# Attention over two caches: one branch's scores turned to keys-by-queries, its row sums taken from a ones column that GpSimd puts beside V

## The chip, the cores and the metric

The kernel runs on one core of one Trainium2 chip. The metric is device time in microseconds, lower is better; the time before is 957.26 us, the median of three runs (957.25 to 958.89).

## What is computed

Two attention blocks, A and B, read their own activations, caches and weights, and their outputs stand side by side. A has 32 query heads on 4 cached heads (8 query heads share one K and V), B has 32 on 32.

```python
def _A_ref(x, k_cache, v_cache, wq, wo):          # B=16, Sq=32, D=1024, Sk=1024, Dh=128
    q = (x @ wq).reshape(B, Sq, Hq, Dh).transpose(0, 2, 1, 3)
    k = jnp.repeat(k_cache, rep, axis=1)          # A: 4 heads, rep = 8;  B: 32 heads, no repeat
    v = jnp.repeat(v_cache, rep, axis=1)
    scores = jnp.einsum("bhqd,bhkd->bhqk", q, k) * (Dh ** -0.5)
    p = _softmax(scores, axis=-1)
    o = jnp.einsum("bhqk,bhkd->bhqd", p, v)
    return o.transpose(0, 2, 1, 3).reshape(B, Sq, Hq * Dh) @ wo
...
return jnp.concatenate([a, b], axis=-1)
```

All tensors are bfloat16. B's K and V are 268 MB together, A's 34 MB, the four weight matrices 34 MB.

## The kernel before

Work is cut into steps, 128 for A and 128 for B. One step of B takes two batches and two heads: 128 rows of queries (2 x 2 x 32) against 1024 keys, with 1 MB of K (`KB_sb`, two buffers) and 1 MB of V (`VB_sb`, three buffers, two loads each). One step of A takes one batch and four of the eight query heads that share a cached head: again 128 rows of queries, on partitions, against 1024 keys. Two steps of A (`half` 0 and 1) use one K and one V of 256 KB (`KA_sb`, `VA_sb`, two buffers each).

A step of A runs so (function `quadA_all`):

1. K is transposed on TensorE through `ps_kt` and copied to `KTA_sb` (`st_ktrA`, L837), once for two steps, for the batch after.
2. `st_scores` (L860): Q is the stationary operand, K-transposed streams by: two matmuls of 512 columns give scores as queries by keys in `ps_s` (two buffers, shared with B).
3. `st_exp` (L899): ScalarE writes exp of the scores to `P_sb` and adds up the rows in `stat` on the way.
4. `st_ptr` (L913): four float32 transposes (two bfloat16 columns taken as one) turn P to keys by queries in `ps_pt`; `st_pev` copies that to `PT_sb` on ScalarE (L588, the helper `evac`).
5. `st_pv` (L931): eight matmuls, one per chunk of 128 keys, add up the output in `ps_o`.
6. `st_recip` (DVE, L950) and `st_norm` (ScalarE, L956) divide by the row sum, giving `O_sb`; `st_otr` transposes it in `ps_o` (L967), and DVE copies it to `OTA_sb` (L590).

B's steps do the same, with K transposed by DVE (`st_ktrB`, L846), scores in small tiles of 32x32 (L882), PV in tiles of 32 columns (L941), the division on DVE (L960) and the last copy on ScalarE. Projections of Q (L657, L674) and of the output (L735) run through the bank `ps_pj`, spread over the steps; sums over blocks of heads are kept in `acc` (L746, L748, L751).

PSUM has eight banks: four for `ps_s`, one each for `ps_kt`, `ps_pt`, `ps_o` and `ps_pj`. Before the change A and B share `ps_pt` and `ps_o`.

The order of instructions is not the order in which the code adds them. Each operation is recorded with what it reads and writes; `list_schedule` then replays all of them with a table of durations (`DUR`) and one figure for the transfer rate (`DMA_BW`), and sorts them by the start that this gives. On the chip each engine works through its own list in that fixed order, with semaphore waits where a buffer demands one. All loads are issued by SyncE (SP), also in a fixed order; a load that waits holds up those behind it. `A_STEPS_FRAC` places A's 128 steps in the first 92% of B's.

The program also holds a second, general version of the computation, which runs only if a check of the row sums fails (`emit_programs`).

Of the kernel before, what the change touches and what calls it, by code (L numbers as in the profile page):

```python
# [7 lines left out]
ALU = alu_op_type.AluOpType  # L8
# [10 lines left out]
A_O_IN_KT = False  # L19
# [16 lines left out]
    "KBt_tr": 1.15, "max": 1.17, "recip": 0.07, "norm@dve": 0.30, "PT_ev@dve": 0.62, "OT_ev@dve": 0.16, "KTA_ev@dve": 0.62,  # L36
# [449 lines left out]
def build(nc, pa, pb, out):  # L486
    P = 128
# [34 lines left out]
    with contextlib.ExitStack() as stack:  # L522
# [10 lines left out]
        stat = sb("stat", [P, 2, 4], F32)  # L533
# [34 lines left out]
        if A_O_IN_KT:  # L568
            OREG = [(ps_kt, BK_KT), (ps_o, BK_O)]
        else:  # L570
            OREG = [(ps_o, BK_O), (ps_o, BK_O)]
# [7 lines left out]
               reads=["z32"], writes=["id32"], name="c1")  # L579

# [141 lines left out]
        def oproj(pi, blk, G):  # L722
# [7 lines left out]
            for oh in range(NOH):  # L730
# [11 lines left out]
                o_ap = ost[:, pi, oh * OUTW:(oh + 1) * OUTW]  # L742
                if nblk == 1:
                    evac(o_ap, ps_pj[:, 0:OUTW], reads=[BK_PJ], writes=[BK_PJ, ("ost", pi)], name="o_fin")
# [15 lines left out]
        def mk_quadA(t):  # L760
# [15 lines left out]
            q.rinv = rinv_all[:, t:t + 1]  # L776
# [38 lines left out]
        def st_dmaV(q):  # L815
            if q.pi == 0:
# [3 lines left out]
                pr.add("sp", lambda e: e.dma_start(VA_sb[:, sl, :, :], pa["v"][q.b, q.s].rearrange("(p c) d -> p c d", c=NCH)),  # L820
# [70 lines left out]
        def st_exp(q):  # L891
# [4 lines left out]
            else:  # L896
# [287 lines left out]
```

## Time and profile before

| | before |
|---|---|
| median of 3 runs | 957.26 us |
| profiled execution | 959.08 us |
| its span | 957.3 us |
| granted TensorE clock, mean | 0.979 |
| busy: DVE / ACT / POOL | 503.5 / 576.0 / 1.3 us |
| DMA packets, share of 16 engines | 94.9% |
| HBM read / written | 337.64 / 2.10 MB |

PE stands for TensorE, PEld for its weight loads, DVE for VectorE, ACT for ScalarE, POOL for GpSimd, SP for SyncE. A row of a group reads: line, engine, operation, what is written and what is read, shape, count, then busy time in us and mean duration in ns, then the engine's idle time ahead of it and what ended most of that. The chain of waits is followed back from the last instruction to whatever released it. A row of waits reads: who waited, for what, us in total, times, the longest. The profile's span is the time from the first to the last instruction on the core.

### The profile page before, as it was taken

To read this page: it belongs to the slowest core of one execution; us is meant where nothing else is said; L and a number is where in the kernel's file an instruction comes from. 1 tells how busy PE (TensorE), PEld (TensorE's weight loads), DVE (VectorE), ACT (ScalarE), POOL (GpSimd) and SP (SyncE) were. 2 spreads that over 40 slices of the span, in tenths; PEclk is the share of its full clock that TensorE was granted. 3 is DMA by queue.
4 is the path that set the end of the run, shared out by engine and by line. 5 is a ranking of instruction groups with operands and counts; after the bars stand their busy time and mean duration, and the time that the engine had idled before them with its cause. 6 is when DMAs were issued, how large, how long until landed. Compare 5 with 4: busy or idle time off the path is not lost.

```text
span 957.3 us, 29084 instructions
## 1 busy us (share of the span) xinstructions
PE 850.0 (89%) x12866; PEld 473.5 (49%) x12866; DVE 503.5 (53%) x955; ACT 576.0 (60%) x1237; POOL 1.3 (0%) x10
## 2 busy tenths in 40 slices
PE   5889999999999899999999899999999988898775
PEld 3345555555555455555555455555555545454332
DVE  1434454545545565555554555654556555556643
ACT  2246676766666666757666666656677656666432
POOL 0000000000000000000000000000000000000000
PEclk7989999999999999999999999999999999999987
DMA  8889999999999999998999999999899999989995
GB/s 318 300 307 369 364 343 367 404 357 360 341 382 388 367 352 352 399 361 318 361 363 408 390 334 370 349 366 389 328 362 378 407 377 358 357 298 363 380 411 179
DMA packets 151938, 341.68 MB, mean 357 GB/s; under 512 B 10496, under 2 KB 26880, under 8 KB 151808
## 3 DMA queue, kind: packets, MB, share of 16 engines
q1 hardware_dynamic: 151808, 339.78, 94.9%
q8 instruction: 102, 1.67, 0.6%
q14 instruction: 28, 0.23, 0.1%
HBM read 337.64 MB, written 2.10 MB: 355 GB/s over the span
## 4 chain that ended last, share of the span: by engine, by line
PE 65%; ACT 24%; DVE 6%; issue 2%; DMA 2%; SPq 0%; POOLq 0%; DVEq 0%
PE ps_pt L913 14%; ACT P_sb L899 13%; PE ps_s L882 12%; PE ps_pj L735 9%; PE ps_o L941 7%; PE ps_pj L657 6%; ACT PT_sb L588 5%; PE ps_pj L674 5%; PE ps_o L931 5%; PE ps_s L860 3%; DVE KBt_sb L846 3%; PE ps_kt L837 2%; ACT QR L588 2%; ACT KTA_sb L588 1%; PE ps_o L967 1%
## 5 line engine op out<-in xcount | busy, mean ns | idle before, releaser
L846 DVE STREAM_TRANSPOSE KBt_sb<-KB_sb 128x1024 f32<-128x1024 f32 x256 | 308.3, 1225 | 38.3 <-PE ps_s L882 27.2
L899 ACT ACTIVATE P_sb<-ps_s 128x1024 bf16<-128x1024 f32 x256 | 263.8, 1030 | 83.3 <-PE ps_s L882 53.7
L588 ACT COPY PT_sb<-ps_pt 128x512 f32<-128x512 f32 x256 | 150.3, 587 | 190.3 <-PE ps_pt L913 169.9
L913 PE MATMUL ps_pt<-id,P_sb 128*128 128x128 f32 x1024 | 184.3, 303 | 24.1 <-ACT P_sb L899 19.5
L913 PEld LDWEIGHTS ps_pt<-id,P_sb 128*128 128x128 f32 x1024 | 147.4, 208 | 76.6 <-ACT P_sb L899 48.4
L882 PE MATMUL ps_s<-KBt_sb,QR 32*32 32x512 bf16 x4096 | 171.0, 400 | 10.5 <-ACT QR L588 8.5
L931 PE MATMUL ps_o<-VA_sb,PT_sb 128*128 128x128 bf16 x1024 | 80.2, 222 | 16.7 <-ACT OTB_sb L588 15.0
L960 DVE TENSOR_SCALAR O_sb<-ps_o,rinv_all 128x128 bf16<-128x128 f32 x128 | 44.1, 345 | 90.4 <-PE ps_o L941 89.7
L941 PEld LDWEIGHTS ps_o<-VB_sb,PT_sb 128*32 128x32 bf16 x4096 | 59.8, 97 | 60.9 <-issue 44.9
L941 PE MATMUL ps_o<-VB_sb,PT_sb 128*32 128x128 bf16 x4096 | 83.9, 222 | 4.9 <-DVE OTA_sb L590 1.8
L950 DVE RECIPROCAL rinv_all<-stat 128x1 f32<-128x1 f32 x256 | 37.9, 150 | 95.8 <-ACT P_sb L899 87.5
L860 PE MATMUL ps_s<-KTA_sb,QT_sb 128*128 128x512 bf16 x256 | 84.9, 384 | 3.6 <-ACT KTA_sb L588 2.0
L931 PEld LDWEIGHTS ps_o<-VA_sb,PT_sb 128*128 128x128 bf16 x1024 | 61.9, 99 | 49.2 <-ACT OTB_sb L588 33.6
L882 PEld LDWEIGHTS ps_s<-KBt_sb,QR 32*32 32x32 bf16 x4096 | 47.4, 89 | 76.9 <-issue 41.1
L735 PE MATMUL ps_pj<-woB_sb,OTB_sb 128*128 128x512 bf16 x256 | 73.1, 386 | 5.4 <-DVE ost L751 2.6
L590 DVE COPY OTA_sb<-ps_o 128x128 bf16<-128x128 bf16 x128 | 27.9, 218 | 93.4 <-PE ps_o L967 92.9
L674 PE MATMUL ps_pj<-wq_sb,xT_sb 128*128 128x512 bf16 x256 | 70.0, 387 | 3.9 <-DMA wq_sb<-in_B_wq_dram 1.7
L735 PE MATMUL ps_pj<-woA_sb,OTA_sb 128*128 128x512 bf16 x256 | 69.7, 380 | 3.4 <-DVE ost L751 1.3
L657 PE MATMUL ps_pj<-xT_sb,wq_sb 128*128 128x512 bf16 x256 | 67.9, 383 | 4.1 <-ACT QR L588 1.3
L748 DVE TENSOR_TENSOR acc<-acc,ps_pj 128x512 f32<-128x512 f32 x64 | 43.8, 684 | 48.9 <-PE ps_pj L735 48.8
L588 ACT CAST QR<-ps_pj 128x256 bf16<-128x256 f32 x128 | 48.5, 379 | 24.0 <-PE ps_pj L694 23.3
L967 PE MATMUL ps_o<-ident,O_sb 128*128 128x128 bf16 x256 | 56.9, 222 | 5.3 <-DVE O_sb L960 2.7
(46 smaller groups left out, 552.2 us busy)
## 6 DMA issues: line engine op xcount, KB each, us to landing
KB_sb<-in_B_k_cache_dram SPq DMA_DIRECT2D x128, 1024.0 KB, 6.9
VB_sb<-in_B_v_cache_dram SPq DMA_DIRECT2D x256, 512.0 KB, 8.0
KA_sb<-in_A_k_cache_dram SPq DMA_DIRECT2D x64, 256.0 KB, 7.2
VA_sb<-in_A_v_cache_dram SPq DMA_DIRECT2D x64, 256.0 KB, 6.5
wq_sb<-in_B_wq_dram SPq DMA_DIRECT2D x32, 256.0 KB, 7.3
wq_sb<-in_A_wq_dram SPq DMA_DIRECT2D x32, 256.0 KB, 7.5
woB_sb<-in_B_wo_dram SPq DMA_DIRECT2D x32, 256.0 KB, 7.7
woA_sb<-in_A_wo_dram SPq DMA_DIRECT2D x32, 256.0 KB, 8.1
```

Of the source, the lines that this page charges most:

```text
L588: pr.add("act", lambda e: e.copy(dst_ap, src_ap), reads=reads, writes=writes, name=name + "@act", wtag=wtag, rtag=rtag)
L657: last = e.matmul(ps_pj[:, 0:tn], wq_sb[:, 0, j, hc * Dh:(hc + 1) * Dh], xT_sb[:, 0, j, t0:t0 + tn], start=(j == 0), stop=(j == DJ - 1))
L674: last = e.matmul(ps_pj[:, 0:CW], xT_sb[:, 1, j, G * P:(G + 1) * P], wq_sb[:, 1, j, :], start=(j == 0), stop=(j == DJ - 1))
L735: last = e.matmul(ps_pj[:, 0:OUTW], OT[:, gp, hh, :], wo_[:, hh, oh * OUTW:(oh + 1) * OUTW], start=(hh == 0), stop=(hh == nh - 1))
L846: pr.add("dve", lambda e: e.transpose(KBt_sb[:, sl, t_, :].bitcast(F32), KB_sb[:, rs, t_, :].bitcast(F32)), reads=[("KB", rs)], writes=[(" ...
L860: pr.add("pe", lambda e, u=u: e.matmul(ps_s[:, sbf, u, :], qt[:, q.b, q.hh0:q.hh0 + 4, :].rearrange("p a q -> p (a q)"), KTA_sb[:, sl, u * ...
L882: last = e.matmul(ps_s[32 * cg:32 * cg + 32, sbf, g2, :].rearrange("p (s j) -> p s j", s=16), lhsT, rhs, start=(fp == 0), stop=(fp == 3), ...
L899: pr.add("act", lambda e: e.activation(dst, src, ACTF.Exp, scale=scale, accum_out=stat[:, sl, 1:2]), writes=BK_S[sbf] + [("P", sl), ("rows ...
L913: last = e.transpose(ps_pt32[:, m * P:(m + 1) * P], p32[:, m:Sk // 2:NPK], id32[:])
L931: last = e.matmul(OREG[0][0][:, 0:Dh], ptc, VA_sb[:, kvs, c, :], start=(c == 0), stop=(c == NCH - 1))
L941: last = e.matmul(ps_o[32 * a:32 * a + 32, 0:Dh], ptc, VB_sb[:, kvs, a // 2, a % 2, c, :], start=(c == 0), stop=(c == NCH - 1), tile_posit ...
L967: pr.add("pe", lambda e: e.transpose(ot_ps, O_sb[:, sl, :], ident[:]), reads=[("O", sl), "ident"], writes=[OREG[q.pi][1]], name="OT_tr", r ...
```

## The change

A's step is cut another way. A step is now one batch, all eight query heads (256 rows of queries) and half of the keys (`half` selects 512 of 1024). K-transposed is the stationary operand and Q streams by, so that scores arrive as keys by queries; exp writes them straight to `PTA_sb` in bfloat16, in the form that PV reads. The transposes `PT_trA`, the copy `PT_ev` and the accumulator of exp are gone for A. V of A is loaded to one buffer `VA_sb`; GpSimd copies it to `VAp_sb` (two buffers), whose rows have 128 columns of V and a column of ones that is set once. PV has 129 columns; the last one is the row sum. Both steps of a batch add up in `ps_kt`; after the second one `st_finA` divides on DVE (reciprocal and product), transposes twice on TensorE and copies once on DVE to `OTA_sb`. A no longer uses `ps_pt` and `ps_o`. B keeps its steps; its `P_sb`, `PT_sb`, `stat` and O lose the index that told A and B apart, as does `ost`, which both now share. Four heads of A's first Q projection (`pro_heads`) come one step of A earlier. The table `DUR` is altered with it.

```diff
 DUR = {
-    "scoresB": 1.1, "scoresA": 0.45, "PT_trA": 0.50, "PT_trB": 0.50, "PVA": 0.48, "PVB": 0.8, "OT_tr": 0.10, "KTA_tr": 0.50,
+    "scoresB": 1.1, "scoresA": 0.45, "PT_trB": 0.50, "PVB": 0.8, "OT_tr": 0.10, "KTA_tr": 0.50,
...
-    "exp": 1.12, "PT_ev@act": 0.52, "norm@act": 0.46, "OT_ev@act": 0.24, "KTA_ev@act": 0.93, "qA_ev@act": 0.52, "qB_ev@act": 0.52,
+    "exp": 1.25, "expA": 1.05, "VAp_cp": 1.2, "normA@dve": 0.42, "OT_trA": 0.2, "OT_evA@dve": 0.35, "PT_ev@act": 0.52, "norm@act": 0.46, "OT_ev@act": 0.24, "KTA_ev@act": 0.93, "qA_ev@act": 0.52, "qB_ev@act": 0.52,
...
-        VA_sb = sb("VA_sb", [P, 2, NCH, Dh], BF)
+        VA_sb = sb("VA_sb", [P, NCH, Dh], BF)
...
+        PTA_sb = sb("PTA_sb", [P, 2, NCH // 2, 2 * P], BF)
+        VAp_sb = sb("VAp_sb", [P, 2, NCH, Dh + 2], BF)
...
+        for i in range(2):
+            pr.add("pool", lambda g, i=i: g.memset(VAp_sb[:, i, :, Dh:Dh + 1], 1.0), writes=[("VAp", i)], name="c0")
...
-                pr.add("sp", lambda e: e.dma_start(VA_sb[:, sl, :, :], pa["v"][q.b, q.s].rearrange("(p c) d -> p c d", c=NCH)),
-                       writes=[("VA", sl)], dma_key=f"va{sl}", name="va_dma", dur=Sk * Dh * 2, wtag={("VA", sl): q.kid})
+                pr.add("sp", lambda e: e.dma_start(VA_sb[:, :, :], pa["v"][q.b, q.s].rearrange("(p c) d -> p c d", c=NCH)),
+                       writes=["VA"], dma_key="va", name="va_dma", dur=Sk * Dh * 2, wtag={"VA": q.kid})
+                pr.add("pool", lambda g: g.tensor_copy(VAp_sb[:, sl, :, 0:Dh], VA_sb[:, :, :]), reads=["VA"], writes=[("VAp", sl)], name="VAp_cp",
+                       rtag={"VA": q.kid}, wtag={("VAp", sl): q.kid})
...
+                qt = QT_sb[:, q.s % 2, q.b, :, :].rearrange("p a q -> p (a q)")
+
+                for c2 in range(2):
+                    def e_st(e, c2=c2):
+                        for i in range(2):
+                            c = 4 * q.half + 2 * c2 + i
+                            last = e.matmul(ps_s[:, sbf, c2, i * 2 * P:(i + 1) * 2 * P], KTA_sb[:, sl, c * P:(c + 1) * P], qt, start=True, stop=True)
+                        return last
...
+                dst = PTA_sb[:, q.half, :, :].rearrange("p c n -> p (c n)")
+                pr.add("act", lambda e: e.activation(dst, src, ACTF.Exp, scale=scale),
+                       writes=BK_S[sbf] + [("PTA", q.half)], name="expA",
...
+        def st_pvA(q):
+            sl, h = q.kvslot, q.half
+
+            def e_pv(e, c0):
+                for c in range(c0, c0 + 2):
+                    for qh in range(2):
+                        last = e.matmul(ps_kt[:, qh * OA0:qh * OA0 + Dh + 1], PTA_sb[:, h, c, qh * P:(qh + 1) * P], VAp_sb[:, sl, 4 * h + c, 0:Dh + 1],
+                                        start=(h == 0 and c == 0 and qh == 0), stop=(h == 1 and c == 3), skip_group_check=True)
+                return last
...
+        def st_finA(q):
+            o2 = ps_kt[:, 0:2 * OA0].rearrange("p (h n) -> p h n", h=2)
+            rinv = rinv_all[:, 2 * q.u:2 * q.u + 2]
+            pr.add("dve", lambda e: e.reciprocal(rinv.rearrange("p (h n) -> p h n", n=1), o2[:, :, Dh:Dh + 1]), reads=[], writes=[BK_KT, "rinvA", ("rinv_all", 0)],
+                   name="recip", rtag={"OpsA": q.kid}, wtag={"rinvA": q.kid})
+            pr.add("dve", lambda e: e.tensor_tensor(OA_sb[:, :, :], o2[:, :, 0:Dh], rinv.rearrange("p (h n) -> p h n", n=1).broadcast_to([P, 2, Dh]), ALU.mult),
+                   reads=["rinvA"], writes=[BK_KT, "OA"], name="normA@dve", rtag={"rinvA": q.kid, "OpsA": q.kid}, wtag={"OA": q.kid})
...
             st_scores(q)
             st_exp(q)
-            st_ptr(q)
-            st_pev(q, "act")
-            st_pv(q)
-            st_recip(q)
-            st_norm(q, "act")
-            st_otr(q, "dve")
+            st_pvA(q)
+            if q.half == 1:
+                st_finA(q)
```

What stands in the engines' lists is set by the replay, so here are rows of those lists: line, operation, what is written and read, shape, and how many of the kind follow each other. First PE before, somewhat before the middle of the program: L882 are B's scores, L941 B's PV, L860 A's scores, L931 A's PV, L913 the transposes of P for A or B, L967 those of O, L657 and L674 Q projections.

```order
L882 MATMUL ps_s<-KBt_sb,QR 32x512 x8
L931 MATMUL ps_o<-VA_sb,PT_sb 128x128 x8
L657 MATMUL ps_pj<-xT_sb,wq_sb 128x512 x2
L913 MATMUL ps_pt<-id,P_sb 128x128 x4
L860 MATMUL ps_s<-KTA_sb,QT_sb 128x512 x2
L967 MATMUL ps_o<-ident,O_sb 128x128
L657 MATMUL ps_pj<-xT_sb,wq_sb 128x512 x6
L882 MATMUL ps_s<-KBt_sb,QR 32x512 x24
L941 MATMUL ps_o<-VB_sb,PT_sb 32x128 x32
L913 MATMUL ps_pt<-id,P_sb 128x128 x4
```

One step of A stands between B's scores. In the changed kernel, at a like place, A's scores are L865, its PV L937, its output transposes L955, K's transposes L839; B's are L887, L971, L992 and L921.

```order
L839 MATMUL ps_kt<-ident,KA_sb 128x128 x8
L674 MATMUL ps_pj<-wq_sb,xT_sb 128x512 x2
L865 MATMUL ps_s<-QT_sb,KTA_sb 128x256 x4
L674 MATMUL ps_pj<-wq_sb,xT_sb 128x512 x2
L971 MATMUL ps_o<-VB_sb,PT_sb 32x128 x32
L937 MATMUL ps_kt<-VAp_sb,PTA_sb 128x129 x8
L992 MATMUL ps_o<-ident,OB_sb 128x128
L937 MATMUL ps_kt<-VAp_sb,PTA_sb 128x129 x8
L865 MATMUL ps_s<-QT_sb,KTA_sb 128x256 x4
L735 MATMUL ps_pj<-woB_sb,OTB_sb 128x512 x2
L955 MATMUL ps_kt<-ident,OA_sb 128x128 x2
L865 MATMUL ps_s<-QT_sb,KTA_sb 128x256 x4
```

No transposes of P are left for A, and three steps of A's scores stand here with no scores of B between them. A dozen rows further on, still on PE of the changed kernel:

```order
L887 MATMUL ps_s<-KBt_sb,QR 32x512 x32
L735 MATMUL ps_pj<-woA_sb,OTA_sb 128x512 x8
L971 MATMUL ps_o<-VB_sb,PT_sb 32x128 x32
L887 MATMUL ps_s<-KBt_sb,QR 32x512 x32
L735 MATMUL ps_pj<-woA_sb,OTA_sb 128x512 x2
L921 MATMUL ps_pt<-id,P_sb 128x128 x4
```

Here two steps of B follow each other with none of A. Last, SP's list, before, with the semaphores that a load waits for in brackets:

```order
L813 DMA KB_sb<-in_B_k_cache_dram 128x2x2048 [waits s_dve]
L808 DMA KA_sb<-in_A_k_cache_dram 128x1024
L826 DMA VB_sb<-in_B_v_cache_dram 128x2x1024 x2
L813 DMA KB_sb<-in_B_k_cache_dram 128x2x2048 [waits s_dve]
L820 DMA VA_sb<-in_A_v_cache_dram 128x1024
L826 DMA VB_sb<-in_B_v_cache_dram 128x2x1024 x2
```

And SP's list of the changed kernel:

```order
L808 DMA KA_sb<-in_A_k_cache_dram 128x1024 [waits s_pe]
L813 DMA KB_sb<-in_B_k_cache_dram 128x2x2048
L820 DMA VA_sb<-in_A_v_cache_dram 128x1024 [waits s_pool]
L813 DMA KB_sb<-in_B_k_cache_dram 128x2x2048 [waits s_dve]
L828 DMA VB_sb<-in_B_v_cache_dram 128x2x1024 [waits s_pe]
L828 DMA VB_sb<-in_B_v_cache_dram 128x2x1024
L808 DMA KA_sb<-in_A_k_cache_dram 128x1024 [waits s_pe]
L820 DMA VA_sb<-in_A_v_cache_dram 128x1024 [waits s_pool]
```

Loads of VA_sb now wait for GpSimd (`s_pool`), and between the two of them stand one load of KB_sb, two of VB_sb and one of KA_sb.

More of the change, by code (lines that the diff above doesn't have):

```diff
@@ L775, in mk_quadA @@
             q.qid = ("A", t)
-            q.rinv = rinv_all[:, t:t + 1]
+            q.u = t // 2
             q.kid = ("A", q.s, q.b)
@@ new lines, in st_pv, with e_pv @@
+        def st_pv(q):
+            kvs = q.vslot
+            def e_pv(e, c0):
+                last = None
+                for c in range(c0, c0 + 2):
+                    for a in range(4):
+                        last = e.matmul(ps_o[32 * a:32 * a + 32, 0:Dh], PT_pairs[:, c // 2, 32 * a:32 * a + 32, c % 2], VB_sb[:, kvs, a // 2, a % 2, c, :],
+                                        start=(c == 0), stop=(c == NCH - 1), tile_position=(0, 32 * a))
+                return last
+            for c0 in range(0, NCH, 2):
+                pr.add("pe", lambda e, c0=c0: e_pv(e, c0), reads=["PT", ("VB", kvs, 0), ("VB", kvs, 1)], writes=[BK_O], name="PVB",
+                       dur=0.2, tag="B%d" % q.t, rtag={"PT": q.qid, ("VB", kvs, 0): q.kid, ("VB", kvs, 1): q.kid}, wtag={"Ops": q.qid})
```

153 lines of the change are left out of this document (59 added, 94 removed).

## The prediction

> **What bounds the kernel now.** I read the busy shares first, then the chain that ended last, then the DMA figures, then all of it by stage.
>
> ```profile
> PE 850.0 (89%) x12866; PEld 473.5 (49%) x12866; DVE 503.5 (53%) x955; ACT 576.0 (60%) x1237; POOL 1.3 (0%) x10
> PE 65%; ACT 24%; DVE 6%; issue 2%; DMA 2%; SPq 0%; POOLq 0%; DVEq 0%
> DMA packets 151938, 341.68 MB, mean 357 GB/s; under 512 B 10496, under 2 KB 26880, under 8 KB 151808
> ```
>
> The first line says that TensorE is busy for 89% of the span and no other compute engine for more than 60%. The second, the chain, runs over PE, ACT and DVE for 95% of the time; transfers end a wait in only 2% of it. So today compute sets the pace. The third line is the warning: 341.68 MB move at 357 GB/s on average, so the queue has not much room either. Three stages and three selected stretches show how much (columns: window, its length, busy us of PE, PEld, DVE, ACT and POOL, then granted clock, DMA share, GB/s):
>
> ```profile
> 0.00:100.00 100.00, 78.42 (x868) 41.05 (x869) 36.46 (x63) 41.95 (x84) 1.18 (x9) 0.90 0.90 327
> 100.00:900.00 800.00, 734.77 (x11288) 414.88 (x11286) 440.99 (x845) 513.92 (x1106) 0.00 (x0) 1.00 0.97 364
> 900.00:957.30 57.30, 36.76 (x713) 17.59 (x713) 26.07 (x49) 20.14 (x47) 0.10 (x1) 0.86 0.82 313
> ...
> 290.00:330.00 40.00, 37.10 (x569) 20.29 (x568) 20.51 (x42) 23.39 (x51) 0.00 (x0) 1.00 1.04 406
> 490.00:530.00 40.00, 36.88 (x544) 21.23 (x544) 21.04 (x42) 25.61 (x58) 0.00 (x0) 1.00 1.05 406
> 735.00:765.00 30.00, 27.51 (x412) 15.12 (x411) 16.98 (x34) 19.63 (x45) 0.00 (x0) 1.00 1.05 407
> ```
>
> The steady stage is 100 to 900. There PE is busy 734.77 of 800 us and idle 65.2, and the queue moves 364 GB/s x 800 us = 291 MB. In three stretches of 30 to 40 us it holds 406 to 407 GB/s, so 406 is a rate that these transfers can sustain. At 406 the steady stage's bytes take 800 x 364 / 406 = **717 us**. Two resources thus stand close together: PE at 735, DMA at 717, and the stage takes 800 because neither is always fed. Start (x and the first weights) and end (B alone, A's steps being over) are stages of their own, and A's attention hardly touches them.
>
> **The change, part by part.** First what leaves PE, ACT and DVE.
>
> ```profile
> L913 PE MATMUL ps_pt<-id,P_sb 128*128 128x128 f32 x1024 | 184.3, 303 | 24.1 <-ACT P_sb L899 19.5 <-ACT PT_sb L588 2.1
> 100.00:900.00 800.00, 166.39 (x932) 133.46 (x930) 1.00 0.97 364
> ...
> L931 PE MATMUL ps_o<-VA_sb,PT_sb 128*128 128x128 bf16 x1024 | 80.2, 222 | 16.7 <-ACT OTB_sb L588 15.0 <-DVE rinv_all L950 1.0 <-DVE OTA_sb L590 0.2
> L860 PE MATMUL ps_s<-KTA_sb,QT_sb 128*128 128x512 bf16 x256 | 84.9, 384 | 3.6 <-ACT KTA_sb L588 2.0 <-DVE QT_sb L590 0.8 <-ACT QT_sb L588 0.7
> 100.00:900.00 800.00, 79.05 (x240) 20.84 (x240) 1.00 0.97 364
> L588 ACT COPY PT_sb<-ps_pt 128x512 f32<-128x512 f32 x256 | 150.3, 587 | 190.3 <-PE ps_pt L913 169.9 <-PE ps_o L941 19.4
> L899 ACT ACTIVATION_READ_ACCUMULATOR P_sb<-ps_s 128x1 f32 x256 | 51.9, 203 | 0.0
> L956 ACT ACTIVATE O_sb<-ps_o,rinv_all 128x128 bf16<-128x128 f32 x128 | 47.7, 373 | 15.1 <-PE ps_o L931 14.3
> L950 DVE RECIPROCAL rinv_all<-stat 128x1 f32<-128x1 f32 x256 | 37.9, 150 | 95.8 <-ACT P_sb L899 87.5 <-ACT O_sb L956 6.8
> L590 DVE COPY OTA_sb<-ps_o 128x128 bf16<-128x128 bf16 x128 | 27.9, 218 | 93.4 <-PE ps_o L967 92.9
> ```
>
> (The two window rows are those of L913 and of L860 alone.) *PE.* Half of the 1024 float32 transposes are A's. In the steady stage 932 take 166.39 us, 0.1785 us each. L860 has 240 of its 256 matmuls there, two for a step, so 120 of A's 128 steps lie there: 120 x 4 x 0.1785 = **86 us less PE work**, leaving 735 - 86 = 649. A's PV (L931) also stops waiting for the shared output bank: its 15.0 us behind OTB_sb go, since A's output moves to the bank of ps_kt.
>
> What PE gets instead is nearly equal. The scores run as 512 matmuls of 256 columns instead of 256 of 512, the same number of columns. The 256 more weight loads cost nothing if each hides behind its neighbour's stream, and 256 x 0.1 us = 26 us if none does (the loads of L860 take 20.84 us for 240, 0.09 each); 649 + 26 is still under 717, so I take zero. PV has 129 columns for 128, 1/128 of 80.2 us: 0.6. The output transposes stay 128.
>
> *ACT* loses 128 x 0.587 (PT_sb) + 128 x 0.373 (norm) + 128 x 0.203 (accumulator read) = 75 + 48 + 26 = 149 us of 576. No ACT work is added, so it becomes an engine with wide gaps.
>
> *DVE* loses 128 x (0.150 + 0.218) = 47 us and gains 64 times a reciprocal, a product of 256 elements and a copy of 256. No row shows those shapes. Neighbours:
>
> ```profile
> L960 DVE TENSOR_SCALAR O_sb<-ps_o,rinv_all 128x128 bf16<-128x128 f32 x128 | 44.1, 345 | 90.4 <-PE ps_o L941 89.7
> L748 DVE TENSOR_TENSOR acc<-acc,ps_pj 128x512 f32<-128x512 f32 x64 | 43.8, 684 | 48.9 <-PE ps_pj L735 48.8
> L590 DVE COPY KTA_sb<-ps_kt 128x1024 bf16<-128x1024 bf16 x33 | 22.6, 685 | 13.6 <-PE ps_kt L837 12.7 <-PE ps_s L860 0.7
> ```
>
> The product lies between 0.345 (128 elements) and 0.684 (512), the copy between 0.218 (128) and 0.685 (1024), the reciprocal at 0.15 or a little more. Low: 64 x 0.71 = 46, high: 64 x 1.52 = 97. I take 57, as 256 lies near the lower ends. DVE goes from 503 to about 513, at most 553: far from a bound.
>
> *GpSimd* gets 64 copies of 128x1024. The engine is idle now; its only priced rows are from the start:
>
> ```profile
> L578 POOL TENSOR_SCALAR_AFFINE_SELECT id<-z 128x128 f32<-128x128 f32 x1 | 0.3, 294 | 0.1
> L574 POOL MEMSET zeros<- 128x128 bf16 x1 | 0.2, 205 | 0.3 <-POOLq L1169 0.3
> L1143 POOL MEMSET ones<- 128x1 f32 x1 | 0.1, 99 | 950.4 <-DVE flag L1142 950.4
> ```
>
> By the memsets an element costs (205 - 99) / 127 = 0.83 ns, by the select (294 - 99) / 127 = 1.53 ns; a copy of 1024 is then 0.95 to 1.67 us. I take 1.67, because the select reads and writes as a copy does: 64 x 1.67 = 107 us in all on an engine that does nothing else.
>
> *The new wait.* V of A now lands in one VA_sb, and the next load of it waits for GpSimd's copy; SP issues in order, so everything behind that load waits too, the loads of B's K and V above all.
>
> ```profile
> VA_sb<-in_A_v_cache_dram SPq DMA_DIRECT2D x64, 256.0 KB, 6.5
> SPq L813 <- DVE KBt_sb L846: 189.4, 54, 13.7
> SPq L820 <- PE ps_o L931: 29.4, 10, 5.3
> ```
>
> A load lands 6.5 us after its issue, plus 1.67 for the copy: the next one can go 8.2 us later. The order rows of SP show in a burst 2304 KB between two VA_sb loads (one VB pair, one KB, one KA, the load itself not counted), 2.36 MB / 406 GB/s = 5.8 us. So SP will stand there. But what it issued behind the first VA_sb load is still queued when that load lands: 5.8 us of transfers cover the 1.67 us of the copy. SP's waits are long today as well (189 us on KBt_sb alone) with the DMA share at 0.97. I cost this wait at nothing; without the cover it would be 64 x 1.67 = 107 us.
>
> *Order.* The new order on PE bunches A's steps: where one step of A stood between two steps of B, the rows now show three steps of A's scores with no scores of B between them, and further on two steps of B with none of A. Within a bunch PE is the busier side, after it the queue is; K has two buffers ahead of the transposes and two behind, V three, so the two sides may drift apart by about one step of B, 2 MB or 5 us, at no cost.
>
> **The sum.** In the steady stage the compute side needs 800 - 86 - 15 = 699 if every other wait stays, the queue 717. The queue is now the longer, by little. What comes on top lies between 0 and 65 us, PE's whole idle time today (800 - 734.77). I take a third, 22: in the three stretches above the queue held 406 beside a PE that was busy for 92 to 93% (37.10 of 40), and PE would now be busy 649 / 717 = 91%, so the rows nearest to the new state show a full queue. Start 100 + 717 + 22 + end 57.3 = 896. The profiled execution took 959.08 us for a span of 957.3, 1.8 beside the span: 898. The median of the runs is 957.26, 1.8 below the profiled one; so **897 us** for the median, 6% less.
>
> **The rivals.**
> *Waits in the fixed order (0.19).* ACT's and DVE's waits remain as they are and PE's 65 us of idle time fall on top of the queue's 717: 100 + 717 + 65 + 57.3 = 939. For it: 95% of the chain is compute, and bunches make the two sides drift. Against it: PE has 68 us to spare under 717.
> *No loss at all (0.07).* 100 + 717 + 57.3 = 874.
> *The rate is already at its ceiling (0.05).* Then the whole span is 341.68 MB at what it moves now, and shorter compute only turns into waits for transfers: 957, no change.
>
> ```profile
> HBM read 337.64 MB, written 2.10 MB: 355 GB/s over the span
> ```
>
> For it stands this row if the mean is the limit; against it the stretches at 406, too long (40 us, 16 MB) to be an effect of buffers. The Trainium skill, "DMA: Bandwidth & Descriptors", section "Where 436 GB/s comes from", has a rule against this change: between HBM and SBUF the limit for a core is about 358 GB/s. By that figure the bytes would take an estimated 954 us and nothing could be won. The trace does not agree, at 406 GB/s over 40 us; the measurement decides.
> *Slower (0.13).* The one VA_sb. If transfers behind a VA_sb load do not cover the copy, since the queue is short at that moment, SP stands still with the DMA engines idle, 64 times. It decides from (957 - 896) / 64 = 0.95 us per load; at the whole 1.67 us the time is 897 + 107 = 1004. For it: SP cannot pass the load, and bunches bring VA_sb loads close together. Against it: the 5.8 us of queued bytes. That the change doesn't do what it says I rule out: the order rows show A's transposes gone.
>
> **How the numbers follow.** Forecast 0.56 (880 to 925, around 897), fixed-order waits 0.19, no loss 0.07, ceiling 0.05, slower 0.13. Faster by over 0.2% (about what a measurement of this kernel can tell from no change): 0.56 + 0.19 + 0.07 = 0.82; within it 0.05; slower 0.13. A range from 874 to 950 takes in the forecast, the fixed-order waits and most of the no-loss case, 0.8; it leaves out the ceiling and the slower case.
>
> **What the profile after would show.** Right: 512 float32 transposes and PE near 765 us busy; ACT near 427; the steady stage's rate from 364 to above 390 GB/s; DMA as releaser in the chain far above 2%; copies on POOL of 0.95 to 1.7 us. Wrong: PE's idle time up with the rate still near 364 (fixed-order waits: look at what ends PE's idle time), or SP's waits on GpSimd's copy with a low DMA share (the one VA_sb), or a rate of 357 with DMA releasing everything (the ceiling). Copies of 3 us or more, or DVE's transposes (1225 ns now) growing longer beside them, would show that GpSimd was priced wrong.

## The result and the profile after

The changed kernel takes **914.95 us** (median of 4 runs, 913.21 to 917.46) against 957.25 for the kernel before (4 runs beside it, 954.77 to 958.89): a ratio of 0.9562, 95% interval 0.9527 to 0.9597. That is 42 us or 4.4% less; 897 had been forecast. The profiled span went from 957.3 to 911.5 us.

First the page of the changed kernel: busy time of the engines, DMA totals, HBM totals, and the chain that ended last.

```profile
PE 783.4 (86%) x12610; PEld 432.9 (47%) x12610; DVE 519.3 (57%) x891; ACT 462.1 (51%) x853; POOL 67.9 (7%) x76
DMA packets 151934, 341.64 MB, mean 375 GB/s; under 512 B 10496, under 2 KB 26880, under 8 KB 151808
HBM read 337.64 MB, written 2.10 MB: 373 GB/s over the span
PE 56%; ACT 14%; DVE 13%; DMA 12%; issue 2%; SPq 2%; POOL 0%; POOLq 0%; DVEq 0%; ACTq 0%
```

The bytes are the same, the mean rate rose from 357 to 375 GB/s, and transfers now end 12% of the chain instead of 2%. ACT's part of the chain fell from 24% to 14%. But PE still leads it: the queue has not taken over as the bound.

The stages, cut at 860 because the end starts earlier now (window, its length, busy us of PE, PEld, DVE, ACT and POOL, granted clock, DMA share, GB/s):

```profile
0.00:100.00 100.00, 77.32 (x800) 37.64 (x800) 34.88 (x56) 34.78 (x58) 6.45 (x16) 0.86 0.85 308
100.00:860.00 760.00, 672.35 (x11144) 378.47 (x11129) 459.60 (x788) 407.11 (x747) 61.38 (x59) 0.98 1.01 388
860.00:911.50 51.50, 33.71 (x685) 16.80 (x681) 24.80 (x47) 20.24 (x49) 0.10 (x1) 0.92 0.81 313
```

In the steady stage the rate is 388 instead of 364 GB/s: 760 us x 388 = 294.9 MB. At 406 these bytes would take 726 us, so **34 us** lie on top of the queue's floor. PE is idle for 88 of the 760 us (760 - 672.35), more than the 65 of 800 before, so it does not bind alone either.

The new and altered groups on PE, DVE, ACT and GpSimd (line, engine, operation, tiles, shape, count, then busy us and mean ns, then idle time ahead and what ended it):

```profile
L921 PE MATMUL ps_pt<-id,P_sb 128*128 128x128 f32 x512 | 91.7, 302 | 18.4 <-ACT P_sb L907 16.9 <-ACT PT_sb L588 1.3
L865 PE MATMUL ps_s<-QT_sb,KTA_sb 128*128 128x256 bf16 x512 | 85.3, 275 | 4.2 <-ACT PTA_sb L901 2.2 <-ACT QT_sb L588 0.7 <-DVE KTA_sb L590 0.3
L937 PE MATMUL ps_kt<-VAp_sb,PTA_sb 128*128 128x129 bf16 x1024 | 80.3, 221 | 5.4 <-ACT KTA_sb L588 2.3 <-DVE KTA_sb L590 1.2 <-ACT PTA_sb L901 1.0
L848 DVE STREAM_TRANSPOSE KBt_sb<-KB_sb 128x1024 f32<-128x1024 f32 x256 | 306.6, 1223 | 46.3 <-DMA KB_sb<-in_B_k_cache_dram 22.6 <-PE ps_s L887 18.9 <-PE ps_o L971 2.4
L949 DVE TENSOR_TENSOR OA_sb<-ps_kt,rinv_all 128x256 bf16<-128x256 f32 x64 | 27.0, 422 | 1.9
L590 DVE COPY OTA_sb<-ps_kt 128x256 bf16<-128x256 bf16 x64 | 17.8, 278 | 25.2 <-PE ps_kt L955 25.2
L947 DVE RECIPROCAL rinv_all<-ps_kt 128x2 f32<-128x2 f32 x64 | 10.4, 162 | 50.4 <-PE ps_kt L937 50.3
L822 POOL COPY VAp_sb<-VA_sb 128x1024 bf16<-128x1024 bf16 x64 | 66.6, 1040 | 770.5 <-DMA VA_sb<-in_A_v_cache_dram 667.3 <-PE ps_kt L937 36.9 <-PE ps_s L865 31.2
```

Most of the predicted mechanics is there. A's 512 float32 transposes are gone, 512 are left (184.3 to 91.7 us). The scores as 512 matmuls take 85.3 us where 256 took 84.9, so the extra weight loads cost that row nothing. OTB_sb is no longer among the waits of A's PV (15.0 us before). DVE's new three cost 0.422 + 0.278 + 0.162 = 0.86 us for a batch, 55 us in all (57 had been taken). GpSimd's copy takes 1.040 us, near the lower end of 0.95 to 1.67, and DVE's transposes stay at 1223 ns (1225 before). By the Trainium skill, "GPSIMD Engine Reference", section "4.1 Engine selection", an operation with one input runs on GpSimd at roughly line rate. 1.040 us for 1024 elements, about 1.02 ns each, fit this loosely: DVE copies as many to `KTA_sb` in 0.685 us in the row of before, though out of PSUM.

SP's longest waits (who waited for what, us in all, times, longest):

```profile
SPq L813 <- DVE KBt_sb L848: 220.4, 64, 13.0
SPq L820 <- POOL VAp_sb L822: 103.5, 33, 5.8
```

SP does stand for GpSimd's copy, 33 times. Whether that costs time needs a run. The wait on KBt_sb is longer than before (189.4), but that row alone misleads. The same load of K is put down to other DVE operations too, before above all to this one:

```profile
SPq L813 <- DVE rinv_all L950: 188.6, 41, 8.9
```

All of L813's rows behind DVE come to 465 us before and to 334 after, so SP stands less at the loads of K than it did. One place shows what such a wait does now. Four windows of 10 us and one of 2 inside the third, then SP's issues and DVE's transposes of K around the poor one (start, length, queue or engine, line, operation, tiles, count; idle time ahead in brackets):

```profile
770.00:780.00 10.00, 9.18 (x189) 6.02 (x174) 7.54 (x14) 5.12 (x11) 1.04 (x1) 1.00 1.04 404
780.00:790.00 10.00, 9.23 (x185) 5.20 (x184) 4.40 (x10) 7.27 (x13) 1.04 (x1) 1.00 1.04 398
790.00:800.00 10.00, 8.51 (x113) 4.66 (x111) 8.13 (x13) 4.26 (x8) 0.00 (x0) 1.00 0.71 247
800.00:810.00 10.00, 8.31 (x161) 4.53 (x161) 5.34 (x8) 3.81 (x10) 0.00 (x0) 0.88 1.04 411
...
792.00:794.00 2.00, 1.90 (x43) 1.35 (x41) 2.00 (x4) 1.46 (x2) 0.00 (x0) 1.00 0.04 11
```

```profile
783.94 0.37 SPq L813 DMA_DIRECT2D KB_sb<-in_B_k_cache_dram  x1
784.35 1.45 SPq L828 DMA_DIRECT2D VB_sb<-in_B_v_cache_dram  x2
793.37 0.37 SPq L813 DMA_DIRECT2D KB_sb<-in_B_k_cache_dram  x1
```

```profile
781.56 2.35 DVE L848 STREAM_TRANSPOSE KBt_sb<-KB_sb 128x1024 f32<-128x1024 f32 x2
...
790.98 2.36 DVE L848 STREAM_TRANSPOSE KBt_sb<-KB_sb 128x1024 f32<-128x1024 f32 x2
```

After its two VB loads, done by 785.8, SP issues nothing until 793.37. It stands at a load of K whose buffer is freed by the transposes that DVE starts at 790.98 and ends at 793.34. The bytes already queued run out some 6 us later: from 792 to 794 the queue moves 11 GB/s, and the slice has 247. On either side it is 398 to 411. PE is busy at 8.5 of 10 us meanwhile. So full rate and stalls alternate.

### The profile page after: what moved, and what is told of

The parts are those of the page before. It is cut to its first block, busy times and chain, and to the rows that moved or that the text cites. A ratio compares the mean times of both kernels' runs of the same rounds, so it can differ in the third digit from the quotient of the medians.

```text
span 911.5 us, 28186 instructions
## 1 busy us (share of the span) xinstructions
PE 783.4 (86%) x12610; PEld 432.9 (47%) x12610; DVE 519.3 (57%) x891; ACT 462.1 (51%) x853; POOL 67.9 (7%) x76
## 4 chain that ended last, share of the span: by engine, by line
PE 56%; ACT 14%; DVE 13%; DMA 12%; issue 2%; SPq 2%; POOL 0%; POOLq 0%; DVEq 0%; ACTq 0%
PE ps_pj L735 10%; PE ps_s L887 10%; DVE KBt_sb L848 6%; PE ps_o L971 6%; PE ps_pj L657 6%; PE ps_pt L921 6%; ACT P_sb L907 5%; PE ps_pj L674 5%; PE ps_kt L937 4%; DMA KB_sb<-in_B_k_cache_dram 4%; ACT PTA_sb L901 3%; PE ps_s L865 3%; DMA wq_sb<-in_A_wq_dram 3%; DVE acc L748 3%; PE ps_kt L839 2%
## 5 line engine op out<-in xcount | busy, mean ns | idle before, releaser
L848 DVE STREAM_TRANSPOSE KBt_sb<-KB_sb 128x1024 f32<-128x1024 f32 x256 | 306.6, 1223 | 46.3 <-DMA KB_sb<-in_B_k_cache_dram 22.6
L887 PE MATMUL ps_s<-KBt_sb,QR 32*32 32x512 bf16 x4096 | 167.0, 402 | 13.8 <-ACT P_sb L907 7.4
L901 ACT ACTIVATE PTA_sb<-ps_s 128x1024 bf16<-128x1024 f32 x128 | 131.6, 1029 | 73.1 <-PE ps_s L865 59.9
L907 ACT ACTIVATE P_sb<-ps_s 128x1024 bf16<-128x1024 f32 x128 | 131.7, 1029 | 70.3 <-PE ps_pt L921 36.5
L588 ACT COPY PT_sb<-ps_pt 128x512 f32<-128x512 f32 x128 | 74.9, 585 | 150.6 <-PE ps_o L971 116.5
L822 POOL COPY VAp_sb<-VA_sb 128x1024 bf16<-128x1024 bf16 x64 | 66.6, 1040 | 770.5 <-DMA VA_sb<-in_A_v_cache_dram 667.3
L921 PE MATMUL ps_pt<-id,P_sb 128*128 128x128 f32 x512 | 91.7, 302 | 18.4 <-ACT P_sb L907 16.9
L987 DVE TENSOR_SCALAR OB_sb<-ps_o,rinv_all 128x128 bf16<-128x128 f32 x128 | 44.4, 347 | 108.0 <-PE ps_o L971 107.6
L921 PEld LDWEIGHTS ps_pt<-id,P_sb 128*128 128x128 f32 x512 | 74.2, 208 | 43.2 <-ACT P_sb L907 25.2
L971 PE MATMUL ps_o<-VB_sb,PT_sb 128*32 128x128 bf16 x4096 | 84.9, 224 | 8.4 <-DMA VB_sb<-in_B_v_cache_dram 6.7
L865 PE MATMUL ps_s<-QT_sb,KTA_sb 128*128 128x256 bf16 x512 | 85.3, 275 | 4.2 <-ACT PTA_sb L901 2.2
L937 PE MATMUL ps_kt<-VAp_sb,PTA_sb 128*128 128x129 bf16 x1024 | 80.3, 221 | 5.4 <-ACT KTA_sb L588 2.3
L971 PEld LDWEIGHTS ps_o<-VB_sb,PT_sb 128*32 128x32 bf16 x4096 | 60.1, 98 | 52.1 <-issue 38.7
L657 PE MATMUL ps_pj<-xT_sb,wq_sb 128*128 128x512 bf16 x256 | 74.0, 406 | 11.4 <-DMA wq_sb<-in_A_wq_dram 4.2
L887 PEld LDWEIGHTS ps_s<-KBt_sb,QR 32*32 32x32 bf16 x4096 | 49.7, 90 | 67.5 <-issue 19.5
L937 PEld LDWEIGHTS ps_kt<-VAp_sb,PTA_sb 128*128 128x128 bf16 x1024 | 64.9, 98 | 31.2 <-issue 13.4
L674 PE MATMUL ps_pj<-wq_sb,xT_sb 128*128 128x512 bf16 x256 | 71.0, 391 | 4.3 <-ACT QR L588 1.8
L865 PEld LDWEIGHTS ps_s<-QT_sb,KTA_sb 128*128 128x128 bf16 x512 | 44.3, 98 | 32.3 <-ACT PTA_sb L901 5.8
```

What stands on the lines that cost most here:

```text
L588: pr.add("act", lambda e: e.copy(dst_ap, src_ap), reads=reads, writes=writes, name=name + "@act", wtag=wtag, rtag=rtag)
L657: last = e.matmul(ps_pj[:, 0:tn], wq_sb[:, 0, j, hc * Dh:(hc + 1) * Dh], xT_sb[:, 0, j, t0:t0 + tn], start=(j == 0), stop=(j == DJ - 1))
L674: last = e.matmul(ps_pj[:, 0:CW], xT_sb[:, 1, j, G * P:(G + 1) * P], wq_sb[:, 1, j, :], start=(j == 0), stop=(j == DJ - 1))
L848: pr.add("dve", lambda e: e.transpose(KBt_sb[:, sl, t_, :].bitcast(F32), KB_sb[:, rs, t_, :].bitcast(F32)), reads=[("KB", rs)], writes=[(" ...
L865: last = e.matmul(ps_s[:, sbf, c2, i * 2 * P:(i + 1) * 2 * P], KTA_sb[:, sl, c * P:(c + 1) * P], qt, start=True, stop=True)
L887: last = e.matmul(ps_s[32 * cg:32 * cg + 32, sbf, g2, :].rearrange("p (s j) -> p s j", s=16), lhsT, rhs, start=(fp == 0), stop=(fp == 3), ...
```

## The experiments

Theory at the outset: PE's work was the bound, the queue is now, and what the kernel loses beyond the queue's floor comes from SP's waits at the K loads. The first rival: the gain came from elsewhere (ACT's relief, the bank), and PE is still the bound. Each ratio is against runs of the kernel before, made beside the run. In the traces of these runs over a hundred matmul records are missing (x12468 of 12610, say), which makes PE's busy time some 20 us too short: b_dma, with the same PE work as the kernel before, shows 828.8 us for 850.0.

**b_pe: three quarters of A's transposes left out, nothing else.**

```diff
-                for m in range(NPK):
+                for m in range(NPK if q.pi else 1):
                     last = e.transpose(ps_pt32[:, m * P:(m + 1) * P], p32[:, m:Sk // 2:NPK], id32[:])
```

> The kernel before, with three of the four float32 transposes left out in A's steps (384 of 1024, so A's part of the output is wrong); ScalarE's copy of P, the banks, the loads and every list stay. PE work falls by 384 x 0.18 = 69 us. Theory (compute paced the kernel before, and the transposes are the greater part of what the change won): 910 to 930 us. Rival (ScalarE's copies or the shared output bank were what counted): 945 us or more.

Measured 930.43 us (928.49 to 931.23), ratio 0.9709 [0.9672, 0.9746]: 26.5 us less. PE's work alone gives over half of the change's gain. But the work left out is less than the 69 us that were expected. Here is the row of the transposes, then the first row of this run's page, and that of b_dma (below), which has all transposes and about as many records missing:

```profile
L913 PE MATMUL ps_pt<-id,P_sb 128*128 128x128 f32 x640 | 138.1, 314 | 26.4 <-ACT P_sb L899 18.9 <-ACT PT_sb L588 5.8 <-issue 0.2
PE 789.9 (85%) x12331; PEld 425.6 (46%) x12482; DVE 502.6 (54%) x955; ACT 576.5 (62%) x1237; POOL 1.3 (0%) x10
PE 828.8 (87%) x12711; PEld 471.8 (49%) x12866; DVE 503.6 (53%) x955; ACT 575.9 (60%) x1237; POOL 1.3 (0%) x10
```

The row falls from 184.3 to 138.1, by 46 us, since one transpose alone takes about 0.36 us where four in a row took 0.72; PE as a whole is busy for 39 us less, since the row overlaps with others. So about 40 us of PE's time bring 26.5.

**b_bank: A's output in its own bank, in the kernel before.**

```diff
-A_O_IN_KT = False
+A_O_IN_KT = True
```

> The kernel before with A's output in the bank of ps_kt (its own switch), nothing else; the planner lays its lists anew. PE waited 15.0 us for the shared bank ahead of A's PV. Theory (that wait goes): 940 to 950 us. Rival (the wait comes back elsewhere): 953 us or more.

Measured 942.65 us (938.63 to 948.53), ratio 0.9859 [0.9812, 0.9907]: 16 us less than the 958.65 beside it, 9 to 18 by the interval. The row of L931 had said 15.0 us behind OTB_sb. The new bank also gives a new order, so the run does not show that this wait alone is the 16 us.

**b_pe_bank: both together.**

> The kernel before with two parts of the change alone: three of the four float32 transposes of P are left out in A's steps (so P's other columns are not transposed and A's output is not the reference's), and A's output has a bank of its own. ACT's copy of PT_sb, its norm and its accumulator stay. Theory: PE's work and the shared bank are the whole gain, and they add up: 26.5 + 16 = 42.5 us off 957.3, so 910 to 920. Rival: ACT's 114 us less carry a part of the gain, and without them the two parts overlap: 922 to 932.

Measured 927.23 us (925.26 to 929.33), ratio 0.9692 [0.9656, 0.9728]: 29.4 us less than the 956.63 beside it, not 42.5. So the two do not add up, and that 26.5 + 16 equals the change's 42.3 is chance. Their chain and stage:

```profile
PE 51%; ACT 21%; DVE 13%; DMA 9%; issue 4%; SPq 1%; DVEq 0%; POOLq 0%; ACTq 0%
100.00:860.00 760.00, 665.74 (x10697) 367.27 (x10837) 436.13 (x835) 506.31 (x1099) 0.00 (x0) 1.00 0.99 378
```

With PE relieved, ACT still holds 21% of the chain and transfers 9%. The other 12 us or so of the change (927.2 to 915.0) come with what this kernel lacks: the last quarter of the transposes, ACT's copies, norms and accumulator reads, and the new order. The runs do not tell these apart.

**b_dma and a_dma: 26.5 MB fewer weights, in the kernel before and in the changed one.** The three loads of weights take 8 of 128 partitions after their first block:

```diff
-                    pr.add("sp", lambda e: e.dma_start(woA_sb[:, h_, :], wo[r0:r0 + Dh, :]),
+                    pr.add("sp", lambda e: e.dma_start(woA_sb[0:(P if s_ == 0 else 8), h_, :], wo[r0:r0 + (P if s_ == 0 else 8), :]),
```

> The kernel before, with the weight loads after the first block of each cut to 8 of 128 partitions (26.5 MB of 341.7 fewer, the output is wrong); planner's lists unchanged. At 406 GB/s that is 65 us of queue time. Theory (compute paced the kernel before): 940 to 957 us. Rival (the queue was the limit already): 895 to 915 us.

> The changed kernel, with the same 26.5 MB of weight loads left out (the output is wrong), lists unchanged. Theory (the queue is now the longer side): 30 to 50 us less, 865 to 885 us, more than the same cut wins in the kernel before. Rival (fixed order): 905 us or more.

b_dma: 957.21 us (955.48 to 958.87), ratio 1.0 [0.9982, 1.0019]. The page of this run:

```profile
DMA packets 131395, 315.14 MB, mean 330 GB/s; under 512 B 9633, under 2 KB 12577, under 8 KB 131265
PE 63%; ACT 24%; DVE 6%; issue 3%; DMA 2%; SPq 0%; POOLq 0%; DVEq 0%
```

Nothing is gained: the rate simply falls to 330 GB/s. So before the change the queue did not set the pace, as its 2% of the chain had said. a_dma: 898.75 us (894.75 to 901.29), ratio 0.9394 [0.9356, 0.9432]: 16 us less than the changed kernel, where 26.5 MB are worth 65 us at 406 GB/s. That lies between the theory (865 to 885) and the rival (905 or more), and neither holds: after the change the queue binds, but for a part of the time only. The chain of this run has DMA at 3% again, and in the steady stage the rate falls:

```profile
PE 62%; ACT 18%; DVE 13%; issue 4%; DMA 3%; SPq 0%; POOLq 0%; DVEq 0%; ACTq 0%
100.00:860.00 760.00, 659.22 (x11182) 381.12 (x11305) 465.07 (x802) 412.03 (x762) 60.34 (x58) 0.98 0.96 363
```

So with transfers mostly out of the way the compute engines and their waits on each other still take 898.75 us, where b_dma has 957.21: the change made this side about 58 us shorter.

**a_pe: the changed kernel with three quarters of B's transposes left out.**

```diff
-                for m in range(NPK):
+                for m in range(1):
```

> The changed kernel, with three of the four float32 transposes left out in B's steps (384 of 512, so B's part is wrong): PE work again 69 us less. Theory (the queue is now the longer side): it wins little, 895 to 912 us. Rival (waits in the fixed order of the compute engines still set the pace): 850 to 880 us.

Measured 906.33 us (902.85 to 911.73), ratio 0.9471 [0.9417, 0.9525]: 8.6 us less than the changed kernel, give or take 6, for the same transposes that were worth 26.5 before. Its row of transposes (91.7 us in the changed kernel), chain and steady stage:

```profile
L921 PE MATMUL ps_pt<-id,P_sb 128*128 128x128 f32 x128 | 44.5, 347 | 17.4 <-ACT P_sb L907 16.6 <-ACT PT_sb L588 0.6
PE 38%; DMA 29%; DVE 16%; ACT 11%; issue 3%; SPq 2%; POOL 0%; DVEq 0%; POOLq 0%; ACTq 0%
100.00:860.00 760.00, 626.04 (x10764) 338.58 (x10878) 462.34 (x793) 409.88 (x754) 60.45 (x58) 0.98 1.02 391
```

Even with PE busy for 626 of 760 us (114 of the stage's records missing) the rate stays at 391, not 406. The row falls by 47 us, and PE as a whole is busy for 728.6 us, 36 less than the 764.6 of a_va2 (below), where about as many records are missing. Cutting PE is worth about a quarter of its size, and so is cutting the queue: neither binds alone.

**a_va2: two buffers of VA_sb in the changed kernel** (the room is made by laying three small tiles of the start and the end over others).

```diff
-        VA_sb = sb("VA_sb", [P, NCH, Dh], BF)
+        VA_sb = sb("VA_sb", [P, 2, NCH, Dh], BF)
...
+                pr.add("pool", lambda g: g.tensor_copy(VAp_sb[:, sl, :, 0:Dh], VA_sb[:, sl, :, :]), reads=[("VA", sl)], writes=[("VAp", sl)], name="VAp_cp",
```

> The changed kernel with two buffers for V of A ahead of GpSimd's copy (room from constants that share other tiles), so that a load no longer waits for the copy of the one before. SP waited 103.5 us for GpSimd in the changed kernel. Theory (the queued transfers cover that wait): no change beyond 5 us, 910 to 919 us. Rival (the wait is the reason why the queue runs at 388 and not 406 GB/s): 895 to 903 us.

Measured 916.57 us (915.09 to 917.38), ratio 0.957 [0.9548, 0.9592], against 0.9562 for the changed kernel: the same. SP's 103.5 us behind GpSimd are down to 2.9, and the first of its waits is still

```profile
SPq L813 <- DVE KBt_sb L848: 232.8, 63, 13.2
```

So the wait for GpSimd was covered, as far as the intervals tell. SP now stands longer at the loads of K instead (384 us behind DVE in all, for 334).

**a_kbh: each 1 MB load of K as two of 512 KB,** so that a half can be loaded as soon as its own transpose is done.

```diff
-                pr.add("sp", lambda e: e.dma_start(KB_sb[:, sl, :, :], ksrc), writes=[("KB", sl)], dma_key=f"kb{sl}", name="kb_dma", dur=4 * Sk * Dh * 2, wtag={("KB", sl): q.kid})
+                for t_ in range(2):
+                    pr.add("sp", lambda e, t_=t_: e.dma_start(KB_sb[:, sl, t_, :], ksrc[:, t_, :]), writes=[("KB", sl, t_)], dma_key=f"kb{sl}_{t_}", name="kb_dma",
```

> The changed kernel with each 1 MB load of B's K as two loads of 512 KB, each with its own semaphore, so that half of a buffer is free after the first of its two DVE transposes; the planner lays its lists anew. SP waited 220 us for KBt_sb. Theory (the queue runs dry while a whole K buffer is held): 10 to 25 us less, 890 to 905 us. Rival (what holds the queue up is the order of compute): 910 us or more.

Measured 917.47 us (913.22 to 924.25), ratio 0.96 [0.9556, 0.9643]: no gain; the rival held. SP's first wait did get shorter:

```profile
SPq L814 <- DVE KBt_sb L850: 143.0, 89, 9.7
```

All of SP's waits for DVE at the loads of K come to 275 us, for 334. Shorter waits there are not enough.

**a_kb3v2: three buffers of K and two of V in the changed kernel.**

```diff
-NVB_SLOTS = 3
-NKB_SLOTS = 2
+NVB_SLOTS = 2
+NKB_SLOTS = 3
```

> The changed kernel with one 1 MB buffer moved from V of B to K of B (three KB_sb, two VB_sb); the replay sets a new order for it. Theory: the dips of the rate come from loads of KB_sb that stand until DVE's transposes free one of two buffers; SP's wait on KBt_sb falls from 220 us to under 120, and a part of the steady stage's 34 us over the queue's floor goes: 893 to 905. Rival: the wait goes over to the loads of VB_sb, which then stand behind PE's PV (28 us before, over 100 now): 912 to 930.

Measured 919.45 us (912.74 to 921.82), ratio 0.9617 [0.9585, 0.965]. SP's waits:

```profile
SPq L828 <- PE ps_s L887: 205.9, 56, 8.8
SPq L828 <- PE ps_o L971: 88.4, 25, 7.3
SPq L820 <- POOL VAp_sb L822: 87.1, 28, 6.5
SPq L813 <- DVE KBt_sb L848: 48.1, 13, 9.8
```

The wait on KBt_sb fell from 220 to 48 us as expected, and the time did not: the loads of V (L828) now wait 294 us behind PE instead of 28. The rival held. A load waits until B's steps have used up what is there. Which buffer it waits at is a matter of how the room is shared out.

**The order alone: a_idx, a_bw and a_mix.** All three have the changed kernel's instructions. a_idx takes, among the operations that can start, the one recorded first (A's steps mostly one by one), and also weighs a switch between PE's tilings five times as much; a_bw gives the replay 406 GB/s; a_mix weighs the recorded place by a little.

```diff
-                ci = max(cand, key=lambda i: (bl[i] - 8.0 * sw(i), -i))
+                ci = max(cand, key=lambda i: (-i - 40.0 * sw(i), bl[i]))
```

```diff
-DMA_BW = 330.7e3
+DMA_BW = 406e3
```

```diff
-                ci = max(cand, key=lambda i: (bl[i] - 8.0 * sw(i), -i))
+                ci = max(cand, key=lambda i: (bl[i] - 0.05 * i - 8.0 * sw(i), -i))
```

> The changed kernel with another rule in the planner for operations that are ready at once: the one recorded first, not the one with the longest way to the end. A's steps then stand one by one between B's, as before the change. Theory (bunched steps of A let the compute side and the queue drift apart): 890 to 908 us. Rival (bunching is absorbed by the buffers): 910 to 920 us; a worse order otherwise: above 920.

> The changed kernel, its replay given 406 GB/s for the transfer rate in place of 330.7; only the order of instructions differs. Theory: the 34 us are the price of this one order, which was laid out for a slower queue than the chip has, so an order laid out for the chip's rate is better by some of them: 895 to 908. Rival: they are the price of any fixed order of these steps: 911 to 922, with SP's wait on KBt_sb still near 220 us.

> The changed kernel with a replay that weighs an operation's place in the program by a little (0.05 us for each operation recorded ahead of it) beside the longest way to the end; only the order differs, with A's steps spread more evenly than in the changed kernel and less than one by one. Theory: the price of the order is not in the bunches as such (one by one cost 57 us more), so a half-way order lies between the two: 915 to 945. Rival: bunches cost and the one-by-one order lost for another reason: 895 to 908.

a_idx: 971.84 us (970.21 to 972.17), ratio 1.0139 [1.0114, 1.0163], 1.4% slower than the kernel before. a_bw: 926.83 us (924.07 to 929.12), ratio 0.968 [0.9641, 0.9719], slower than both ranges named for it. a_mix: 912.78 us (910.26 to 916.44), ratio 0.9541 [0.9499, 0.9583], the same as the changed kernel and between the two ranges named for it, so it settles neither. Two waits of ACT in a_idx, which in the changed kernel are 28.1 us (on B's scores) and 15.8 us (on O's transposes):

```profile
ACT P_sb L907 <- PE ps_s L887: 174.3, 110, 4.6
ACT OTB_sb L588 <- PE ps_o L992: 134.7, 114, 3.3
```

And the chain and two waits of DVE in a_bw:

```profile
PE 44%; DMA 29%; DVE 17%; ACT 6%; issue 4%; SPq 1%; DVEq 0%; POOLq 0%
```

```profile
DVE KBt_sb L848 <- DMA KB_sb<-in_B_k_cache_dram: 103.0, 46, 6.1
DVE OB_sb L987 <- PE ps_o L971: 61.6, 61, 3.3
```

In a_idx ACT waits for B's scores at 110 of 128 exps, against 30 in the changed kernel, and the theory that bunches of A's steps cost time did not hold. That these waits are the 57 us is likely but not shown, as ACT's row of waits is not on its own a price. In a_bw the order counts on transfers at 406 GB/s at every moment, and DVE, queued up for K that is not there yet, waits 103 us where it waited 22.6; the theory that a planner with the true rate does better fell as well. With equal work, four orders span 913 to 972 us, more than the whole change. None of the runs that do the whole computation beats the changed kernel by more than the intervals.

## Why the prediction came out as it did

The direction and the range held, and so did what leaves the engines, the price of GpSimd's copy and its cover. The balance of the two sides did not: by a_dma the compute side, not the queue, is still the longer. The time is 18 us over the forecast, and it lies in the range partly by luck: 717 + 22 = 739, meant as a queue that is not always fed, happens to come close to a compute side of some 742 that had been taken as 699. By the steps:

- *PE's transposes, 86 us off the steady stage.* The count was right, the price was not: the time of a row counts what overlaps with PE's other rows. The matmul rows of before sum to 1032.6 us where the page has 850.0, those of after to 935.7 where it has 783.4. In the trace of before, PE without the instructions of L913 is busy for 721.7 us, so all 1024 transposes add 128 us to it and not 184.3; A's half adds 64, about 60 in the steady stage. PE over all went down by 66.6, to 783.4 and not 765.
- *The compute side at 699, the queue the longer.* This step failed. a_dma puts the shortening of the compute side at about 58 us, where 86 + 15 = 101 were taken. If all of it falls in the steady stage, an estimate, the stage needs 800 - 58 = 742 us on this side, more than the queue's 717.
- *The shared bank, 15 us.* About right in itself (16 us alone), but not on top of the transposes: together the two brought 29 us, less than their sum.
- *The queue's floor.* Right that it is near and can be sustained: the steady rate rose to 388 GB/s ("above 390" was just missed), and DMA from 2% to 12% of the chain. The rival of a ceiling at 357 is refuted. By the Trainium skill, "DMA: Bandwidth & Descriptors", section "Where 436 GB/s comes from", a core is held to about 358 GB/s; the 388 GB/s of the steady stage do not agree.
- *What comes on top, 22 us: mis-sized.* Measured are 34 us over 726. By a_dma some 16 of them go when the queue gets room; the others then are the compute side's own length, 742 against 726. The reason given, stretches in which the queue held 406 beside a PE busy for 92%, read the best 30 to 40 us as the new state. In the changed kernel such stretches still alternate with slices at 250 to 360, in which SP stands at a load. The rival that put all 65 us on top is 24 us too long, but the pace that it rests on, that of the compute engines, still makes up 83% of the chain (PE, ACT and DVE).
- *Start taken as unchanged.* It moves 308 instead of 327 GB/s, 1.9 MB less in 100 us; these bytes have to move later.
- *The one VA_sb at nothing.* Right: a second buffer changes the time by less than the intervals.
- *ACT to 427, and no path through it.* It went to 462. The three rows that leave sum to 149, but rows of ACT overlap: its twelve rows of before sum to 662 us where the page has 576.0, its twelve of after to 512 where it has 462.1. As on PE, a row's busy time must not be taken off the engine's. That ACT counts for nothing is not shown either, as b_pe_bank left 12 us to it and to others.
- *Bunches at no cost.* Not contradicted: a slightly more even order (a_mix) takes the same time, and A's steps mostly one by one (a_idx) take 57 us more.

The sum of the miss in the span (911.5 against 896.3): the steady stage had 294.9 MB to move instead of 291.2, 9 us; the loss in it was 34 instead of 22, 12 us; the end window is 51.5 us long instead of 57.3, 6 us less; 9 + 12 - 6 = 15 us. Of the 3.7 MB more, 1.9 come over from the start; the other 1.8 belong to the shorter end window, whose cut lies 40 us earlier.

For the start, here is the chain between 40 and 60 us (start, length, what), and the window after it:

```profile
42.62 1.61 PE ps_pj L657 x7
44.23 5.30 DMA wq_sb<-in_A_wq_dram
49.53 0.05 issue
49.58 1.73 PE ps_pj L657 x4
...
52.07 3.61 PE ps_pj L657 x8
```

```profile
50.00:60.00 10.00, 8.48 (x19) 2.20 (x18) 0.71 (x2) 0.59 (x1) 0.00 (x0) 0.50 1.01 390
```

In the chain A's Q projection waits 5.3 us for weights, and in the ten microseconds behind it the granted clock is 0.50. PE itself does not stand still all that time; four matmuls of the same line run in it, after this gap (start, length, what; idle time ahead in brackets):

```profile
47.90 1.31 PE L657 MATMUL ps_pj<-xT_sb,wq_sb 128*128 128x512 bf16 x4 [3.32 <-DMA wq_sb<-in_A_wq_dram]
```

Eight matmuls of L657 take 3.61 us at 52.07, where seven took 1.61 at 42.62. The Trainium skill, "TensorE: Matmul & The Clock Gate", section "HAM oscillation — how this bites in real kernels", says that PE-idle gaps over about 3.4 us bring the throttle back. The longest gap here, 3.32 us, lies just under that, so this place neither bears the rule out nor refutes it. The earlier Q projections alone do not force a poor start: a_idx has them too, and its first 100 us move 334 GB/s.

```profile
0.00:100.00 100.00, 75.61 (x854) 38.72 (x863) 37.07 (x59) 36.42 (x62) 6.53 (x17) 1.00 0.91 334
```

What the order around them adds was not taken apart.

**What stays open:** which single wait makes up the 34 us, and how the last 12 us of the gain divide. It is not GpSimd's copy (a_va2), not the size of a K load (a_kbh), and not the number of K buffers at equal room (a_kb3v2). With less PE work it shrinks a little (a_pe: 391 GB/s, 297.2 MB, 28 us over the floor). With fewer bytes (a_dma) the time falls, but the stage lies 80 us over its lower floor (275.9 MB at 406 GB/s are 680 us). That points to a compute side and a queue of nearly the same length, coupled in a fixed order with hardly any room between them; it is argued and not shown. More room for K and V together would be the test, and it was not tried for want of SBUF.

## What to carry to other kernels

Where two resources stand within a few per cent of each other, the gain of relieving one is neither its own work nor the way down to the other's floor: here about 40 us of PE work were worth 26.5 us before and 8.6 us after, and savings measured one by one (26.5 and 16) brought 29 together. Do not take a row's busy time off its engine's: what a group adds to the engine is what no other row covers, 128 of 184 us here. Take as loss over the floor what the stage as a whole loses, not what its best stretches do. Before touching buffers, lay out the same work in two or three other orders, since that alone moved the time by 59 us.

## What the runs showed of the hardware that had not been expected

GpSimd copies 128x1024 in bfloat16 in 1.040 us, near the lower of the two prices that its own rows of the start gave, and with DVE's transposes at an unchanged mean (1223 ns against 1225). Taking 26.5 MB off the queue changed the time of the kernel before by nothing that the runs can tell (ratio 0.9982 to 1.0019), though the DMA engines showed a share of 0.97 in its steady stage: a share near one is no proof that transfers are waited for.
